# A scheduler that writes the order of work for one core: new durations, a lock between two engines, and one load per block

## The chip, the core and the metric

The kernel runs on one core of a Trainium2 chip. The core has five engines that each run their own list of instructions in the order in which the program was built: TensorE (PE, matrix products; its weight loads are shown as PEld), VectorE (DVE), ScalarE (ACT), GpSimd (POOL) and SyncE (SP), which here only issues DMAs. ACT issues some DMAs too, on a queue of its own. An engine waits when its next instruction needs a result that is not there yet, and everything behind that instruction on the same engine waits with it. The metric is the device time of one execution in microseconds (us), as the median of several runs.

## What is computed

Queries, keys and values are float32, the weights float64; the result is float32. First an attention over 4 batches, 8 heads, 576 positions and 64 values a head, which is the sum of a pooled part (queries, keys and values averaged in groups of four, 144 by 144 scores a head) and a local part (each position sees its neighbours at a distance under four). Then two feed-forward stages on 2304 tokens. In short:

```python
out_d = sm_attn(q_d, k_d, v_d)             # pooled by 4
out_up = np.repeat(out_d, factor, axis=2)
mask = np.abs(pos[:, None] - pos[None, :]) < factor
out_local = softmax(where(mask, q @ k.T / 8, -1e9)) @ v
x = out_up + out_local                     # 2304 x 512
h = x @ w_in                               # 512 -> 2048
x = (h * np.cos(h)) @ w_out                # 2048 -> 512
a = x @ w1;  b = x @ w2                    # 512 -> 1024
out = (a * b @ w3) @ w_out2                # 1024 -> 1024 -> 512
```

## The kernel before

The program is not written in the order in which it runs. It consists of small jobs (generators), each with an urgency, that ask for one operation after the other on a named engine. The function `run` (line 271) plays the kernel through once while it is being built: it keeps a clock, and whenever an engine is free it gives it the most urgent operation whose inputs are visible. `cost` (line 89) says how long an operation takes, `LATENCY` (line 67) how long until others see its result. The order of instructions that comes out of this game is what the chip then runs. So a change of a number in `cost` changes no operation; it changes which operation stands where in an engine's list.

The stages, by the names that the trace shows:

- Start: a batch's blocks of queries and keys are loaded (tiles `qb` and `kb`); two constants, `bands_in` and `ident_in`, come over ACT's own DMA queue (lines 1094 to 1096) and are turned into `ident_r` (line 1100), which the first local scores `ps_sb` need. Pooled sums `qkd` are made on VectorE and give the pooled scores `ps_s`. While TensorE has nothing to do, the scheduler puts products of zeros into its list (`ps_z`, and later into `ps_w`; `warm_up`, line 1058).
- `ps_w`: w3 times the last weights, 64 float32 products. The weights come as float64, and `w_job` (line 315) makes float32 of them: an ACT activation `t<-raw`, a VectorE shift `t<-t`, a VectorE or `w<-raw,t`; for later stages also an ACT copy and a GpSimd subtraction (`wi`, `wo`).
- `ps_h` and `ps_y`: the first feed-forward stage, 96 steps of 12 products each in both; between them `chain_job` (line 801) computes h cos h on ACT, VectorE and GpSimd. The attention of the later batches is threaded in: `ps_s`, `ps_t`, `ps_p` for the pooled part (`pair_job`, line 455), `ps_sb`, `ps_tb`, `ps_av` for the local part (`unit_job`, line 592; a unit is two blocks of 96 positions).
- `ps_ab` and `ps_o`: the second stage.

The functions that the change touches are `cost`, the `issue` inside `Engine`, `unit_qk_job` (line 417: loads for the first batch) and `unit_job` (line 592: loads for the other batches, and the scores).

Of the kernel before, what the change touches and what calls it, by code (L numbers as in the profile page):

```python
# [21 lines left out]
P = 128  # L22
# [10 lines left out]
KB = QB + 2 * HALO  # L33
NQB = S // QB
# [24 lines left out]
AHEAD = 12  # L59
A0, A1 = 6.0, 6  # L60
# [6 lines left out]
LATENCY = {"pe": 200, "se": 140, "ve": 130, "ge": 150, "sy": 2450}  # L67
# [9 lines left out]
def fused_kernel(ctx: ExitStack, tc: tile.TileContext, qk_block, v_block, qk_pool, v_pool,  # L77
# [6 lines left out]
    written, table = {}, [AF.Exp]  # L84

    def size(a):
        return math.prod(a.shape[1:])

    def cost(name, op, out, ins, func):
        n = max(size(a) for a in [out] + ins)  # L90
        if name == "ve":
            shared = n > 64 and ends["ge"] > max(now[0], ends["ve"])
            if op.startswith("tensor_scalar") and len(ins) == 1:
                return 90 + n * (1.5 if shared else 0.65)
            both = len(ins) == 2 and n > 64 and not any(a.tensor.name.startswith("ps_") for a in ins)
            return 75 + n * (2.2 if both and shared else 1.17 if both else 1.04)
        if name == "se":
            load = 1283 if func in (AF.Exp, AF.Sin) and func != table[0] else 0
            table[0] = func if load else table[0]
            return (60 if ins[0].tensor.name.startswith("ps_") else 100) + n / 1.2 + load  # L100
        if name == "ge":
            return 160 + (1.7 if any(0 in [step for step, _ in a.ap] for a in ins) else 2.3) * n
        if name == "sy":
            return max(450, n * out.shape[0] * (8 if out.dtype == I64 else 4) / 290)
        n = size(out)
        if op == "transpose":
            return 70
        if ins[0].dtype == F32R:
            return 12.5 + n / 2.4
        quarters = ins[0].shape[0] == D and size(ins[0]) == D  # L110
        return (4 if ins[0].shape[0] == P else 1 if quarters else 2) * max(35, n / 2.4)
# [6 lines left out]
    class Engine:  # L118
# [3 lines left out]
        def __getattr__(self, op):  # L122
            call = getattr(self.engine, op)

            def issue(*args, **kw):
# [9 lines left out]
                end = ends[self.name] = max(now[0], ends[self.name]) + cost(self.name, op, out, ins, kw.get("func")) + (0 if also is None else 183)  # L135
# [75 lines left out]
    def on(name, fn, *aps, when=lambda: True):  # L211
        yield name, fn, aps, when
# [203 lines left out]

    def unit_qk_job(u):
# [3 lines left out]
        unit_qk[u] = qs, ks  # L421
# [7 lines left out]
        yield from on("ve", lambda: ve.tensor_reduce(out=pooled[:, :, 0, ub * n:(ub + 1) * n], in_=qs[1].rearrange("p n (g r) -> p n g r", r=4), axis=AX.X, op=ALU.add), qs[1])  # L429
        for side in range(2):  # L430
            g = ub * n + side * n // 2
            yield from on("ve", lambda: ve.tensor_reduce(out=pooled[:, :, 1, g:g + n // 2], in_=ks[1][:, side, :KC * KB].rearrange("p (n k) -> p n k", n=KC)[:, :, HALO:HALO + QB].rearrange("p n (g r) -> p n g r", r=4), axis=AX.X, op=ALU.add), ks[1])
        count(("pooled", b))
# [158 lines left out]
    def unit_job(u):  # L592
# [8 lines left out]
        if early:  # L601
            yield from until(lambda: u in unit_qk)
            qk_slots, (qs, ks) = zip(*unit_qk.pop(u))
        else:
            qk_slots = yield from take("raw", 2)
            qs, ks = buf(qk_slots[0], "qb", [KC, UQ]), buf(qk_slots[1], "kb", [2, 512])
            for side in range(2):
                yield from on("sy", lambda: sy.dma_start(out=qs[:, :, side * QB:(side + 1) * QB], in_=qk_block[2 * u + side, :, :KC * QB].rearrange("p (n q) -> p n q", n=KC)))
            yield from on("sy", lambda: sy.dma_start(out=ks[:, :, :KC * KB], in_=qk_block[2 * u:2 * u + 2, :, KC * QB:].rearrange("b p n -> p b n")))
# [3 lines left out]
        def scores():  # L613

            for s0, s1, kind in masks_of(u):
# [4 lines left out]
                for side in range(s0, s1):  # L620
                    for m in range(2):
                        for w in range(2):
                            for c in range(2):
                                for r in range(2):
                                    rs, o = slice(r * D, (r + 1) * D), ((side * 2 + m) * 2 + w) * KS
                                    q0, k0 = side * QB + w * (QB - KS), (2 * m + c) * KB + w * (KB - KS)
                                    pe.matmul(ps[r][c * KS:(c + 1) * KS, o:o + KS], lhsT=qs[rs, 2 * m + c, q0:q0 + KS], rhs=ks[rs, side, k0:k0 + KS],
                                              start=u >= BANDS, stop=u >= BANDS or (side, m, w) == (s1 - 1, 1, 1))

        yield from on("pe", scores, qs, ks, bands, ident_r)  # L630
# [558 lines left out]
```

## Time and profile before

| what | value |
|---|---|
| median of 3 runs | 844.81 us (844.55 to 844.94) |
| the profiled execution, device time | 845.89 us |
| its span, first to last instruction | 844.1 us, 15707 instructions |
| PE busy | 827.9 us, 98% of the span |
| DVE, ACT, POOL busy | 517.3, 451.1, 372.7 us |
| granted TensorE clock, mean | 0.997 of full speed |
| DMA | 121.88 MB in 61403 packets, 18960 of them under 512 B |
| table loads on ACT | 28 of 1283 ns |

The span is the stretch that the profile covers; the device time of the same execution is 1.79 us longer, and that execution was 1.08 us above the median. Busy times of the engines overlap each other and don't add up to the span. In a timeline row a group of equal instructions that follow each other is merged; neighbouring groups on PE overlap by 0.1 to 0.2 us, since products are pipelined. A float32 product shows up as two records.

### The profile page before, as it was taken

The page shows a single profiled execution, that of the slowest core. Times are in us where ns is not written, and L with a number is a line of the kernel's source. Part 1 is how long each engine was busy: PE and PEld are TensorE (multiplying, and loading weights), DVE is VectorE, ACT ScalarE, POOL GpSimd, SP SyncE. Part 2 cuts the span into 40 slices and gives each one's busy share as a digit, 9 for nine tenths or more (in the row PEclk, how much of TensorE's full clock was granted, in tenths as well). Part 3 has the DMA queues.
Part 4 walks back from the last instruction along what each step waited for, and adds up shares of the span by engine and source line. Part 5 has one row for each costly group of instructions (what it writes and reads, how often), then busy time and mean ns, then how long its engine had stood idle before and what let it go on. Part 6 is the DMA issues. An engine that isn't in the chain of part 4 may idle for free.

```text
span 844.1 us, 15707 instructions
## 1 busy us (share of the span) xinstructions
PE 827.9 (98%) x5982; PEld 751.1 (89%) x5982; DVE 517.3 (61%) x924; ACT 451.1 (53%) x906; POOL 372.7 (44%) x330
## 2 busy tenths in 40 slices
PE   8999999999999999999999999999999999999997
PEld 7544599999989999999999999999999899999996
DVE  6888789998777678757453442654436544463342
ACT  2646698877778767857775565551214211231111
POOL 0102559865454533634443433444435632363332
PEclk9999999999999999999999999999999999999999
DMA  9997897134453545353332144968002400020102
GB/s 271 295 316 269 278 309 289 40 116 130 139 162 136 187 126 171 106 164 103 103 124 99 64 140 156 365 223 339 26 14 62 138 26 25 26 88 26 26 26 75
DMA packets 61403, 121.88 MB, mean 144 GB/s; under 512 B 18960, under 2 KB 26384, under 8 KB 61328
## 3 DMA queue, kind: packets, MB, share of 16 engines
q1 hardware_dynamic: 54432, 112.12, 41.0%
q10 hardware_dynamic: 6896, 8.76, 3.0%
q8 instruction: 47, 0.77, 0.4%
q14 instruction: 28, 0.23, 0.1%
HBM read 93.07 MB, written 27.79 MB: 143 GB/s over the span
## 4 chain that ended last, share of the span: by engine, by line
PE 81%; DVE 8%; DMA 6%; ACT 3%; issue 1%; POOL 1%; ACTq 0%; DVEq 0%; POOLq 0%
PE ps_ab L138 20%; PE ps_y L138 18%; PE ps_h L138 18%; PE ps_o L138 12%; PE ps_w L138 7%; DVE t L138 3%; DMA raw<-w_out 2%; PE ps_t L138 2%; DVE c L138 1%; DMA raw<-w_in 1%; PE ps_av L138 1%; PE ps_tb L138 1%; PE ps_sb L138 1%; PE ps_s L138 1%; DMA vr<-v_pool 1%
## 5 line engine op out<-in xcount | busy, mean ns | idle before, releaser
L138 PE MATMUL ps_y<-g,wo 128*128 128x384 f32 x1152 | 221.2, 337 | 0.5 <-POOL g L138 0.5
L138 PE MATMUL ps_h<-xs,wi 128*128 128x384 f32 x1152 | 220.6, 337 | 1.1 <-POOL wi L138 1.1
L138 PEld LDWEIGHTS ps_h<-xs,wi 128*128 128x128 f32 x1152 | 200.1, 188 | 5.2 <-issue 2.4
L138 PEld LDWEIGHTS ps_y<-g,wo 128*128 128x128 f32 x1152 | 199.9, 188 | 3.0 <-issue 1.4
L138 PE MATMUL ps_ab<-y,w 128*128 128x384 f32 x1008 | 185.1, 336 | 0.9 <-DVE v L138 0.8
L138 PEld LDWEIGHTS ps_ab<-y,w 128*128 128x128 f32 x1008 | 176.8, 188 | 6.5 <-issue 1.4
L138 DVE TENSOR_TENSOR v<-v,ps_ab 128x384 f32<-128x384 f32 x168 | 90.8, 552 | 136.8 <-ACT w L138 70.4
L138 POOL TENSOR_TENSOR g<-c,g 128x384 fp32r<-128x384 f32 x96 | 108.5, 1131 | 137.6 <-ACT g L138 125.6
L138 ACT ACTIVATE c<-c 128x384 f32<-128x384 f32 x192 | 100.4, 523 | 30.1 <-DVE c L138 27.6
L138 POOL TENSOR_TENSOR v<-v 128x384 f32<-128x384 f32 x48 | 49.8, 1039 | 140.9 <-DVE v L138 139.1
L138 PE MATMUL ps_o<-w,m 128*128 128x512 f32 x432 | 107.3, 392 | 0.0
L138 ACT CAST m<-v 128x384 fp32r<-128x384 f32 x48 | 24.5, 514 | 141.0 <-POOL v L138 141.0
L138 DVE SCALAR_TENSOR_TENSOR c<-turns,ps_h 128x384 f32<-128x384 int32 x96 | 52.6, 548 | 67.1 <-ACT turns L138 61.0
L138 PEld LDWEIGHTS ps_o<-w,m 128*128 128x128 f32 x432 | 80.3, 188 | 14.1
L138 DVE SCALAR_TENSOR_TENSOR c<-c,ps_h 128x384 f32<-128x384 f32 x96 | 52.6, 548 | 45.5 <-ACT c L138 45.2
L138 ACT ACTIVATE turns<-ps_h 128x384 int32<-128x384 f32 x96 | 47.0, 489 | 42.9 <-PE ps_h L138 42.6
L138 ACT CAST g<-c 128x384 fp32r<-128x384 f32 x96 | 49.2, 512 | 37.3 <-DVE c L138 31.3
L138 PE MATMUL ps_w<-w,w 128*128 128x512 f32 x128 | 61.1, 617 | 1.0 <-DVE w L138 1.0
L138 DVE TENSOR_SCALAR t<-t 128x512 int32<-128x512 int32 x72 | 49.7, 704 | 10.0 <-ACT t L138 10.0
L138 ACT ACTIVATE t<-raw 128x512 f32<-128x512 f32 x72 | 47.7, 675 | 13.9 <-DMA raw<-w 6.0
L138 POOL TENSOR_TENSOR m<-v,m 128x384 fp32r<-128x384 f32 x48 | 47.8, 1017 | 0.0
L138 POOL TENSOR_TENSOR xs<-xb,xs 128x384 fp32r<-128x384 f32 x24 | 26.9, 1122 | 47.2 <-ACT xs L138 47.1
(89 smaller groups left out, 866.3 us busy)
## 6 DMA issues: line engine op xcount, KB each, us to landing
w_sc<-w SPq DMA_DIRECT2D x56, 256.0 KB
w<-w_sc SPq DMA_DIRECT2D x28, 512.0 KB
raw<-w SPq DMA_DIRECT2D x24, 512.0 KB
raw<-w3t SPq DMA_DIRECT2D x16, 512.0 KB
raw<-w_in SPq DMA_DIRECT2D x16, 512.0 KB
raw<-w_out SPq DMA_DIRECT2D x16, 512.0 KB
qkr<-qk_pool SPq DMA_DIRECT2D x12, 576.0 KB
vb<-v_block SPq DMA_DIRECT2D x48, 128.0 KB
```

The lines of the kernel that those rows point to most:

```text
L138: return call(*args, **kw)
```

## The change

Three things are changed.

1. A block's queries and keys (they lie side by side in DRAM, 792 values per partition) come in one DMA into one tile `qk`, where before queries of two blocks went into `qb`, 96 values at a time, by two DMAs, and keys of two blocks into `kb` by a third. The function `halves` gives the two views of the new tile. In the first batch each VectorE sum of `qkd` over 768 values becomes two over 384.
2. The table in `cost`, the latencies and the DMA rate have other numbers. One line of it stands here for all.
3. The scheduler's game knows a lock between VectorE and GpSimd (`held`): a GpSimd `tensor_tensor` and a VectorE operation that works from SBUF to SBUF with two inputs (or a `tensor_scalar`) wait for each other there. It also adds a price for TensorE's change between products with few and with many rows. These are prices in the game; no instruction is added for them.

```diff
+QK = KC * (QB + KB)
+RATE = 310
-LATENCY = {"pe": 200, "se": 140, "ve": 130, "ge": 150, "sy": 2450}
+LATENCY = {"pe": 200, "se": 145, "ve": 115, "ge": 120, "sy": 2450}
+    def held(name, op, out, ins, start):
+        if name == "ge" and op == "tensor_tensor":
+            return max(0.0, lock["ve"] - 60 - start)
+        if name == "ve" and size(out) > 64 and on_chip(out) and all(on_chip(a) for a in ins) and (len(ins) == 2 or op.startswith("tensor_scalar")):
+            return max(0.0, lock["ge"] - 110 - start)
+        return None
-            return 160 + (1.7 if any(0 in [step for step, _ in a.ap] for a in ins) else 2.3) * n
+            return (160 + 1.66 * n) if any(0 in [step for step, _ in a.ap] for a in ins) else 132 + 2.18 * n
...
-                end = ends[self.name] = max(now[0], ends[self.name]) + cost(self.name, op, out, ins, kw.get("func")) + (0 if also is None else 183)
+                start = max(now[0], ends[self.name])
+                wait = held(self.name, op, out, ins, start)
+                if self.name == "pe":
+                    part = op == "matmul" and ins[0].shape[0] <= QP and ins[0].dtype == F32
+                    start += 0 if part == parts[0] else 120 if part else 200
+                    parts[0] = part
+                end = ends[self.name] = start + (wait or 0) + cost(self.name, op, out, ins, kw.get("func")) + (0 if also is None else 190)
+                if wait is not None:
+                    lock[self.name] = end
...
-        qs = yield from load(lambda t: [(t[:, :, side * QB:(side + 1) * QB], qk_block[2 * u + side, :, :KC * QB].rearrange("p (n q) -> p n q", n=KC)) for side in range(2)], "w", ANY, "qb", (KC, UQ), F32)
-        ks = yield from load(lambda t: [(t[:, :, :KC * KB], qk_block[2 * u:2 * u + 2, :, KC * QB:].rearrange("b p n -> p b n"))], "w", ANY, "kb", (2, 512), F32)
+        for side in range(2):
+            got.append((yield from load(qk_block[2 * u + side], "w", ANY, "qk", (QK,), F32)))
...
+            g, (qs, ks) = ub * n + side * n // 2, halves(got[side][1])
+            for which, src in enumerate((qs, ks[:, :, HALO:HALO + QB])):
+                yield from on("ve", lambda: ve.tensor_reduce(out=pooled[:, :, which, g:g + n // 2], in_=src.rearrange("p n (g r) -> p n g r", r=4), axis=AX.X, op=ALU.add), src)
```

The order of instructions changes on every engine. Over the whole program TensorE keeps its 76 products `ps_z` and loses the 12 products of zeros `ps_w<-zeros`; the other products are the same in number. The table loads on ACT become 20. The places that matter below:

First place, VectorE while the second unit's scores come in (`sc` are local scores, `bmax` their maxima or sums, `nm` and `sums` and `sd` belong to a pooled pair, `vr` and `vd` to pooled values, `t` and `w` to weights). Before:

```order
L138 TENSOR_TENSOR vr<-vr 72x2x256
L138 TENSOR_TENSOR sc<-ps_sb,bmax 128x512
L138 TENSOR_TENSOR vd<-vr 72x256
L138 TENSOR_REDUCE bmax<-ps_sb 128x8
L138 TENSOR_REDUCE nm<-ps_s 72x2 x2
L138 TENSOR_REDUCE bmax<-sc 128x16
L138 TENSOR_SCALAR nm<-nm 72x4
L138 TENSOR_SCALAR t<-t 128x512
```

and now:

```order
L160 TENSOR_TENSOR vr<-vr 72x2x256
L160 TENSOR_REDUCE bmax<-ps_sb 128x8
L160 TENSOR_TENSOR vd<-vr 72x256
L160 TENSOR_TENSOR sc<-ps_sb,bmax 128x512
L160 TENSOR_REDUCE bmax<-ps_sb 128x8
L160 TENSOR_SCALAR t<-t 128x512
L160 TENSOR_TENSOR sc<-ps_sb,bmax 128x512
L160 TENSOR_REDUCE nm<-ps_s 72x2 x2
L160 TENSOR_REDUCE bmax<-sc 128x16
L160 TENSOR_SCALAR nm<-nm 72x4
L160 SCALAR_TENSOR_TENSOR w_323<-raw,t 128x512
```

The subtraction `sc<-ps_sb,bmax` of the second unit's first half now stands ahead of `nm`, and the first weight's `or` ahead of the division of `bmax`.

Second place, VectorE right behind that, up to the second weight, which the first `ps_w` needs. Before:

```order
L138 TENSOR_SCALAR bmax<-bmax 128x16
L138 RECIPROCAL bmax<-bmax 128x16
L138 SCALAR_TENSOR_TENSOR w_342<-raw,t 128x512
L138 TENSOR_SCALAR t<-t 128x512
L138 TENSOR_SCALAR sums<-sums 72x4
L138 RECIPROCAL sums<-sums 72x4
L138 SCALAR_TENSOR_TENSOR w_361<-raw,t 128x512
L138 TENSOR_TENSOR sd<-sd,sums 72x576
```

and now:

```order
L160 TENSOR_SCALAR bmax<-bmax 128x16
L160 RECIPROCAL bmax<-bmax 128x16
L160 TENSOR_SCALAR t<-t 128x512
L160 TENSOR_REDUCE bmax<-ps_sb 128x8
L160 TENSOR_SCALAR sums<-sums 72x4
L160 RECIPROCAL sums<-sums 72x4
L160 TENSOR_REDUCE nm<-ps_s 72x2
L160 TENSOR_TENSOR sd<-sd,sums 72x576
L160 TENSOR_REDUCE nm<-ps_s 72x2
L160 SCALAR_TENSOR_TENSOR w_358<-raw,t 128x512
```

Two `nm`, one `bmax` and the product `sd<-sd,sums` have moved ahead of the second weight's `or`.

Third place, TensorE from the first `ps_w` on. Before:

```order
L138 MATMUL ps_w_375<-w_342,w_361 128x512
L138 MATMUL ps_w_389<-w_342,w_361 128x512
L138 MATMUL ps_w_394<-w_342,w_361 128x512
L138 MATMUL ps_w_400<-w_342,w_361 128x512
L138 MATMUL ps_w_375<-zeros 128x256
L138 MATMUL ps_t<-ident,sd 72x72 x8
L138 MATMUL ps_tb<-ident,sc 128x128 x8
L138 MATMUL ps_w_375<-zeros 128x256 x5
L138 MATMUL ps_t<-ident,sd 72x72 x8
L138 MATMUL ps_t<-ptp,vd 64x144 x4
L138 MATMUL ps_s<-qkd 72x144 x4
L138 MATMUL ps_w_375<-zeros 128x256
```

and now:

```order
L160 MATMUL ps_w_394<-w_323,w_358 128x512
L160 MATMUL ps_t<-ident,sd 72x72 x8
L160 MATMUL ps_w_403<-w_323,w_358 128x512
L160 MATMUL ps_tb<-ident,sc 128x128 x8
L160 MATMUL ps_s<-qkd 72x144 x4
L160 MATMUL ps_w_428<-w_323,w_358 128x512
L160 MATMUL ps_t<-ident,sd 72x72 x8
L160 MATMUL ps_t<-ptp,vd 64x144 x4
L160 MATMUL ps_w_467<-w_323,w_358 128x512
L160 MATMUL ps_w_394<-w_409,w_423 128x512
L160 MATMUL ps_s<-qkd 72x144 x4
```

The twelve products of zeros in this stretch are gone (seven of them stand in the rows of before), and transposes and pooled scores stand between the first products `ps_w`.

## Rows read from the trace of the kernel before

**Rows 1.** Stretches: us, busy us of PE, PEld, DVE, ACT, POOL; PEclk, DMA share, GB/s
```profile
0.00:24.00 24.00, 18.63 (x227) 16.14 (x227) 15.79 (x29) 7.39 (x17) 2.80 (x7) 0.99 0.97 266
24.00:104.00 80.00, 80.00 (x637) 42.12 (x637) 67.71 (x150) 48.69 (x132) 20.13 (x14) 0.98 0.91 293
104.00:155.00 51.00, 49.20 (x348) 46.56 (x347) 45.92 (x68) 46.94 (x93) 40.28 (x29) 1.00 0.77 255
155.00:200.00 45.00, 43.14 (x363) 41.98 (x362) 42.61 (x60) 35.20 (x67) 31.85 (x23) 1.00 0.30 91
200.00:560.00 360.00, 358.31 (x2963) 345.71 (x2962) 220.63 (x401) 246.81 (x477) 162.58 (x145) 1.00 0.45 146
560.00:840.00 280.00, 278.64 (x1454) 258.57 (x1452) 124.53 (x220) 65.73 (x123) 115.02 (x113) 1.00 0.22 77
```

**Rows 2.** What PE waited for: us in total, times, longest us
```profile
PE ps_sb L138 <- DVE sc L138: 1.3, 1, 1.3
PE ps_tb L138 <- DVE sums L138: 1.3, 1, 1.3
PE ps_sb L138 <- ACT ident_r L138: 1.1, 1, 1.1
PE ps_h L138 <- POOL wi L138: 1.1, 2, 0.8
```

**Rows 3.** PE in order of time: start us, us, operation, idle before it
```profile
23.90 5.24 PE L138 MATMUL ps_w<-w,w 128*128 128x512 f32 x8 [1.01 <-DVE w L138]
30.39 0.84 PE L138 MATMUL ps_w<-zeros 128*128 128x256 f32 x5
31.07 0.67 PE L138 MATMUL ps_t<-ident,sd 72*72 72x72 f32 x8
31.66 0.71 PE L138 MATMUL ps_t<-ptp,vd 72*64 72x144 f32 x8
40.66 4.89 PE L138 MATMUL ps_w<-w,w 128*128 128x512 f32 x11
```

**Rows 4.** The first 24 us on ACT, DVE and POOL in order of time
```profile
0.74 2.62 ACTq L132 DMA_DIRECT2D bands_raw<-bands_in  x4
8.46 0.31 ACT L138 ACTIVATE ident_r<-ident 128x128 fp32r<-128x128 f32 x1
11.06 0.69 DVE L138 TENSOR_REDUCE bmax<-ps_sb 128x8 f32<-128x512 f32 x1 [1.24 <-PE ps_sb L138]
19.62 0.42 DVE L138 TENSOR_SCALAR t<-t 128x512 int32<-128x512 int32 x1
20.55 2.15 POOL L138 TENSOR_TENSOR sc<-sc,bmax 128x1024 f32<-128x1024 f32 x1 [19.37 <-DVE bmax L138]
20.87 2.12 DVE L138 TENSOR_SCALAR t<-t 128x512 int32<-128x512 int32 x1
23.19 0.66 DVE L138 SCALAR_TENSOR_TENSOR w<-raw,t 128x512 int32<-128x512 int32 x1
```

**Rows 5.** VectorE's groups: count, busy us, mean ns, idle before
```profile
L138 DVE TENSOR_REDUCE nm<-ps_s 72x2 f32<-72x288 f32 x32 | 13.7, 448 | 10.2 <-PE ps_s L138 10.1
L138 DVE TENSOR_TENSOR sd<-sd,sums 72x576 f32<-72x576 f32 x8 | 6.0, 749 | 0.0
L138 DVE TENSOR_TENSOR sc<-ps_sb,bmax 128x512 f32<-128x512 f32 x4 | 2.7, 680 | 0.0
```

**Rows 6.** DMA queues, 566.8 to 574 us: packets, MB, share of 16 engines
```profile
q1 hardware_dynamic: 600, 2.19, 74.5%
q10 hardware_dynamic: 575, 0.79, 29.4%
```

**Rows 7.** Three stretches at the start, columns as in rows 1
```profile
1.70:4.20 2.50, 2.50 (x13) 2.50 (x13) 0.00 (x0) 0.00 (x0) 0.00 (x0) 1.00 0.94 194
23.60:27.00 3.40, 3.10 (x4) 1.51 (x5) 3.40 (x9) 1.64 (x6) 0.00 (x0) 0.50 1.02 324
24.00:60.00 36.00, 36.00 (x282) 19.64 (x283) 30.91 (x71) 20.63 (x56) 1.90 (x1) 0.96 1.03 309
```

More of the change, by code (lines that the diff above doesn't have):

```diff
@@ L83, in fused_kernel, with on_chip @@
     ends = {"ve": 0.0, "se": 0.0, "pe": 0.0, "ge": 0.0, "sy": 0.0}
-    written, table = {}, [AF.Exp]
+    written, table, lock, parts = {}, [AF.Exp], {"ve": 0.0, "ge": 0.0}, [False]
     def size(a):
         return math.prod(a.shape[1:])
+    def on_chip(a):
+        return not a.tensor.name.startswith("ps_")
+    def held(name, op, out, ins, start):
[4 more added lines that the diff above has]
+        return None
     def cost(name, op, out, ins, func):
@@ L91, in cost @@
         if name == "ve":
[L92 to L96, printed above, removed]
+            if n <= 64:
+                return 80 if op != "tensor_scalar_add" else 190
+            if len(ins) == 1 and op.startswith("tensor_scalar") and on_chip(ins[0]):
+                return 68 + 0.52 * n
+            return 64 + 1.043 * n
         if name == "se":
-            load = 1283 if func in (AF.Exp, AF.Sin) and func != table[0] else 0
+            load = 1290 if func in (AF.Exp, AF.Sin) and func != table[0] else 0
             table[0] = func if load else table[0]
-            return (60 if ins[0].tensor.name.startswith("ps_") else 100) + n / 1.2 + load
+            return (45 if not on_chip(ins[0]) else 128 if func == AF.Prelu else 90) + n / 1.2 + load
         if name == "ge":
-            return 160 + (1.7 if any(0 in [step for step, _ in a.ap] for a in ins) else 2.3) * n
+            return (160 + 1.66 * n) if any(0 in [step for step, _ in a.ap] for a in ins) else 132 + 2.18 * n
         if name == "sy":
-            return max(450, n * out.shape[0] * (8 if out.dtype == I64 else 4) / 290)
+            return max(450, n * out.shape[0] * (8 if out.dtype == I64 else 4) / RATE)
         n = size(out)
         if op == "transpose":
-            return 70
+            return 109 if out.shape[0] == P else 62
         if ins[0].dtype == F32R:
-            return 12.5 + n / 2.4
+            return 13.3 + n / 2.4
         quarters = ins[0].shape[0] == D and size(ins[0]) == D
-        return (4 if ins[0].shape[0] == P else 1 if quarters else 2) * max(35, n / 2.4)
+        return (4 if ins[0].shape[0] == P else 1 if quarters else 2) * max(30, n / 2.4)
     def visible(a):
@@ L602, in unit_job @@
             yield from until(lambda: u in unit_qk)
-            qk_slots, (qs, ks) = zip(*unit_qk.pop(u))
+            qk_slots, qk = zip(*unit_qk.pop(u))
         else:
             qk_slots = yield from take("raw", 2)
-            qs, ks = buf(qk_slots[0], "qb", [KC, UQ]), buf(qk_slots[1], "kb", [2, 512])
+            qk = [buf(slot, "qk", [QK]) for slot in qk_slots]
             for side in range(2):
-                yield from on("sy", lambda: sy.dma_start(out=qs[:, :, side * QB:(side + 1) * QB], in_=qk_block[2 * u + side, :, :KC * QB].rearrange("p (n q) -> p n q", n=KC)))
-            yield from on("sy", lambda: sy.dma_start(out=ks[:, :, :KC * KB], in_=qk_block[2 * u:2 * u + 2, :, KC * QB:].rearrange("b p n -> p b n")))
+                yield from on("sy", lambda: sy.dma_start(out=qk[side], in_=qk_block[2 * u + side]))
+        qs, ks = zip(*(halves(t) for t in qk))
         ns = yield from banks(2)
@@ L625, in scores @@
                                     rs, o = slice(r * D, (r + 1) * D), ((side * 2 + m) * 2 + w) * KS
-                                    q0, k0 = side * QB + w * (QB - KS), (2 * m + c) * KB + w * (KB - KS)
-                                    pe.matmul(ps[r][c * KS:(c + 1) * KS, o:o + KS], lhsT=qs[rs, 2 * m + c, q0:q0 + KS], rhs=ks[rs, side, k0:k0 + KS],
+                                    q0, k0 = w * (QB - KS), w * (KB - KS)
+                                    pe.matmul(ps[r][c * KS:(c + 1) * KS, o:o + KS], lhsT=qs[side][rs, 2 * m + c, q0:q0 + KS], rhs=ks[side][rs, 2 * m + c, k0:k0 + KS],
                                               start=u >= BANDS, stop=u >= BANDS or (side, m, w) == (s1 - 1, 1, 1))
-        yield from on("pe", scores, qs, ks, bands, ident_r)
+        yield from on("pe", scores, *qk, bands, ident_r)
         for s in qk_slots:
```

8 lines of the change are left out of this document (4 added, 4 removed).

## The prediction

> **What bounds the kernel now.** I first read the table by stretches [rows 1]: the reader is to see that TensorE (PE) is busy for all of 24 to 104 us, for 49.20 of 51 us and 43.14 of 45 us in the two stretches behind that, and nearly always from 200 us on. Its idle time is 5.37 us before 24 us, then 1.80, 1.86, 1.69 and 1.36 us. No other engine comes near it over the whole, though VectorE is busy for 42.61 of 45 us from 155 to 200 us, and ACT for 46.94 of 51 us from 104 to 155 us. The products of after are those of before, apart from twelve products of zeros. So the time can move in three ways only: the moment from which PE has real work without a break, the products of zeros, and the 6.7 us of idle time (1.80 + 1.86 + 1.69 + 1.36) behind 24 us. Then I read what PE waited for [rows 2]: single waits of 0.3 to 1.3 us on results of VectorE, ACT and GpSimd, none directly on a DMA. Last I read the start in order of time [rows 3, 4], since the two places of the change that touch it, the loads and VectorE's order, both stand before the first `ps_w` at 23.90 us.
>
> **The start, VectorE's order.** In before the first maximum `bmax<-ps_sb` starts at 11.06 us, when PE's first scores are there [rows 4], and VectorE works without a break until the second weight's `or`, which starts at 23.19 and takes 0.66 us; PE starts `ps_w` with it [rows 3, 4]. The change moves four operations ahead of that `or`. First the subtraction `sc<-ps_sb,bmax` (0.68 us, about 0.6 behind its neighbour), and the first `or` ahead of the division, which shifts the second `t<-t` by about 0.7 in all. Then the lock: in before the second `t<-t` starts at 20.87, just after GpSimd began a 2.15 us product at 20.55, and takes 2.12 us, against 0.42 us for the same operation at 19.62 [rows 4]. From its start to the end of the `or` are 3.0 us. In the new order it follows the division directly and gets in first, 0.4 us; but `sd<-sd,sums`, which has two inputs in SBUF, now stands behind it and must wait out the 2.15 us; with its own 0.75, half of a pair of `nm` (0.45 each) and the `or`, 0.66, that is 4.3 us from the start of `t` [rows 4, 5]. So +0.7 and +1.3: the first `ps_w` starts about 2.0 us later, at 25.9 us, if the scores come as early as before.
>
> **The start, the first rows of zeros and transposes.** From 23.90 to 40.66 us PE works through two rounds of four products `ps_w` and what is between them, 16.8 us [rows 3]. Of this the new order lacks the products of zeros (five step from 30.39 to 31.07, 0.14 each, twelve are 1.6 us), and one pair of `ps_t` and `ps_t<-ptp`, 1.2 us, which comes later instead. In before the clock was at 0.50, the lower of its two levels (1.2 GHz), from 23.6 to 27.0 us [rows 7]: eight records of `ps_w` took 5.24 us, against 4.89 for eleven at 40.66 [rows 3], so about 1.6 us were lost. If the clock holds in after, the stretch takes 16.8 - 1.6 - 1.2 - 1.6 = 12.4 us and the third round starts at 25.9 + 12.4 = 38.3, where before, with the pair taken off, stood at 39.5. That is 1.2 us won; since VectorE also has to finish the third round's weights by then, with one more wait for the lock, I take 1.0.
>
> **The start, the loads.** The first scores need `ident_r`, which ACT makes at 8.46 us, as soon as its constants have landed [rows 4]; PE waited 1.1 us for it [rows 2]. These constants come on ACT's queue in 896 rows of 128 to 384 B (four DMAs of 192 rows, then 96 and 32), 56 on each of 16 DMA engines, beside SP's queue. Where both queues were full, from 566.8 to 574 us, they moved 600 and 575 packets: as many of the one as of the other, though a row of SP's was more than twice as large [rows 6]. In before SP's rows at the start are 384 and 1632 B long, and the DMA engines move 194 GB/s; with rows of 2 KB and more they move 309 GB/s [rows 7]. After the change SP's rows are 3168 B, five times the mean of before (811 KB in 1280 rows for two blocks), and SP's queue never runs dry, as each DMA has 128 rows instead of 256 to 512. If each of the 56 rows takes turns with one of SP's, the constants wait for 56 x 16 x (3168 + 256) B = 3.07 MB at 309 GB/s, 9.9 us from about 2.4 us on (the first of the four is issued from 0.74 to 1.4 us, and SP's first bytes too moved about 1 us behind their issue), and some 0.4 to land. `ident_r` would be made at 12.7 instead of 8.46, 4.2 us later. The other bound is zero: the queue of constants is not held up at all; better than now can't pay, as VectorE's sums fill that time. No row of before shows rows of 3168 B beside these, so the value is an estimate; I take 3.3, as the equal counts are the nearest row. The loads themselves land earlier, by 2.4 MB x (1/194 - 1/309) = 4.6 us at most, but that buys nothing here, since VectorE then stands before `bmax<-ps_sb` with six sums done and must wait for PE.
>
> The Trainium skill, "DMA: Bandwidth & Descriptors", section "Queues, rings and completion order", says that a DMA engine takes turns between queues by whole packets of some 9 to 17 descriptors. By that rule the six DMAs of constants would each wait for one share of a block, 8 rows on each engine, 1.3 us; with 0.7 us for their own bytes that is 8.6 us instead of 9.9, a delay near 2.9 us and a sum lower by 0.4. Counts as in these rows can't tell the two apart.
>
> Start in sum: -1.0 + 3.3 = +2.3 us for all that follows, since PE has no gap until 104 us in which it could catch up.
>
> **The stretch from 104 to 200 us.** The 3.66 us of idle time here are waits for `wi`, `g` and freed banks behind VectorE, ACT and GpSimd, which are nearly full because they convert weights [rows 1, 2]. Their work does not hang on PE's start, so with PE 2.3 us later they are ahead by about that much. I take 2.2 of the 3.66 us back. The 20 table loads instead of 28 take 10 us from ACT, which helps in the same place and counts in it. **From 200 us on** the order is new but of the same kind; of 3.05 us idle I take 0.4 off, with bounds of 1.5 to both sides, since the two long waits there (1.3 us for `sums` is one) may go or come again. The chain at the end is unchanged: the last ten or eleven products `ps_o` cover the last weights' chain in both. The larger loads of later units are hidden, PE waits for no load there now; without that cover each would cost what it lands late, some tenths. The six sums more on VectorE at the start add 6 x 0.05 us at most, and lie before `bmax`.
>
> **Sum.** Against the profiled execution's 845.89 us: +2.3 - 2.2 - 0.4 = 845.6; that execution was 1.08 us above the median, so the forecast for the median is 844.5 us. A measurement of this kernel tells about 0.2%, 1.7 us, from no change; this is no change.
>
> **Rivals.**
> - Faster: the constants land as early as now (delay 0). For it: the new SP DMAs issue fewer rows, so the queue of constants may be served sooner; against it: the equal counts of rows 6. Then -1.0 - 2.2 - 0.4 = -3.6 us, 841.2 us; if all waits behind 104 us went too, 837 us. Chance 0.30.
> - Slower, by one mechanism: the constants come late, PE runs out of zeros at 7 us and stands until 12 us, and as after its half-idle stretch before 23.6 us it gets the lower clock for its first real work. For it: the drop in rows 7; against it: the first real work is mostly paced by VectorE, not by PE. Price: delay 4.2, scores at half clock 1.2, first `ps_w` at half clock 1.6: -1.0 + 4.2 + 2.8 - 2.6 = +3.4, 848.2 us. It decides from delay and clock together above 5.3 us. Chance 0.18.
> - The new order makes waits of its own: after 155 us the second `ps_sb` stands closer behind the first, before VectorE has freed its banks, which cost 1.3 us once already. Twice that more than forecast: 847.1 us. Chance 0.10.
> - The table does nothing on the chip: the lock is still there, the game only knows of it. Then the waits behind 104 us stay as they are and the sum is +2.3, 847.1; a part of this lies in the forecast's spread, and no chance of its own is given.
>
> **How the numbers follow.** Forecast 0.42, the rivals 0.30, 0.18 and 0.10. The forecast's own range is 842.3 to 846.5. The range over all cases goes from 840.8, which takes in half of the faster rival's cases, to 848.4, which takes in the slower ones but the worst. Faster 0.31, same 0.41, slower 0.28: the faster rival and a sliver of the forecast's tail, the forecast, and the two slower ones.
>
> **What would show it.** `ident_r` on ACT at 11 to 13 us instead of 8.46, with an idle time of 3 us or more on PE before the first `ps_sb`; the first `ps_w` at 28 to 30 us and no product of zeros behind it; `sd<-sd,sums` locked beside GpSimd's product instead of `t<-t`; PE idle for under 2 us between 104 and 200. It would be wrong if `ident_r` stands at 9 us (then faster), or if the first `ps_w` starts after 31 us or the granted clock falls to the lower level in the scores (then slower).

## The result, and the profile after

The changed kernel takes 850.13 us in the median of 6 runs (849.11 to 852.48), the kernel before 844.88 (844.55 to 845.61): a ratio of 1.0062, with a 95% interval of 1.0049 to 1.0075. It is slower by 0.6%; 844.5 and no change had been forecast. The profiled execution of after took 849.11 us with a span of 847.2, 3.1 us more than that of before.

The table by stretches, columns as in [rows 1], is that of after. Two single rows follow it: the time from the first `ps_h` to the end, first in before, then in after.

```profile
0.00:24.00 24.00, 19.47 (x215) 16.90 (x215) 14.09 (x30) 6.52 (x15) 0.98 (x7) 0.86 0.93 296
24.00:104.00 80.00, 77.89 (x637) 41.09 (x634) 77.46 (x159) 51.50 (x139) 26.72 (x18) 1.00 0.92 303
104.00:155.00 51.00, 46.44 (x332) 43.87 (x331) 43.65 (x61) 42.16 (x85) 37.11 (x27) 1.00 0.61 223
155.00:200.00 45.00, 44.60 (x374) 43.69 (x373) 40.82 (x62) 34.92 (x67) 30.62 (x23) 1.00 0.29 93
...
```
```profile
103.97:844.10 740.13, 729.33 (x5122) 692.86 (x5120) 433.79 (x748) 395.08 (x758) 349.74 (x309) 1.00 0.38 124
```
```profile
106.48:847.20 740.72, 728.51 (x5106) 692.43 (x5104) 424.67 (x737) 382.07 (x742) 344.88 (x306) 1.00 0.36 121
```

The reader is to see three things. PE's granted clock over the first 24 us is 0.86 instead of 0.99. From 104 to 155 us PE is idle for 51 - 46.44 = 4.56 us instead of 1.80, and from 155 to 200 us for 0.40 instead of 1.86. And the 3.1 us split at the first `ps_h`: it comes 2.5 us later, 0.8 us less work is left behind it, and PE is idle 12.2 us from there to the end instead of 10.8. So in this execution 1.7 us were lost before and 1.4 us behind that product.

What PE waited for, as in [rows 2]. The two waits of 1.3 us for VectorE are gone, those for `ident_r` and the second weight `w` are about 1 us longer, and waits for ACT (`up`, `pt`) are new:

```profile
PE ps_tb L160 <- ACT up L160: 2.2, 1, 2.2
PE ps_w L160 <- DVE w L160: 2.1, 1, 2.1
PE ps_sb L160 <- ACT ident_r L160: 2.0, 1, 2.0
...
PE ps_h L160 <- ACT pt L160: 1.1, 1, 1.1
```

The start in order of time (ACT, then VectorE and GpSimd, then PE), which answers to [rows 3, 4]:

```profile
9.13 0.31 ACT L160 ACTIVATE ident_r<-ident 128x128 fp32r<-128x128 f32 x1 [0.58 <-DMA ident<-ident_in]
...
12.92 0.69 DVE L160 TENSOR_REDUCE bmax<-ps_sb 128x8 f32<-128x512 f32 x1 [4.48 <-PE ps_sb L160]
...
23.45 0.36 DVE L160 TENSOR_SCALAR t<-t 128x512 int32<-128x512 int32 x1
...
24.32 1.29 DVE L160 TENSOR_SCALAR sums<-sums 72x4 f32<-72x4 f32 x1
...
26.09 0.74 DVE L160 TENSOR_TENSOR sd<-sd,sums 72x576 f32<-72x576 f32 x1
...
27.12 0.68 DVE L160 SCALAR_TENSOR_TENSOR w<-raw,t 128x512 int32<-128x512 int32 x1
...
23.68 1.91 POOL L160 TENSOR_TENSOR sc<-sc,bmax 128x1024 f32<-128x1024 f32 x1 [22.49 <-DVE bmax L160]
...
9.49 0.53 PE L160 MATMUL ps_sb<-bands,ident_r 128*128 128x256 f32 x2 [1.97 <-ACT ident_r L160]
...
27.85 1.13 PE L160 MATMUL ps_w<-w,w 128*128 128x512 f32 x2 [2.10 <-DVE w L160]
```

And ACT beside PE behind 102 us, where no row of before stood:

```profile
103.54 0.35 ACTq L146 DMA_DIRECT2D w_sc<-w  x1
104.12 1.06 ACT L160 ACTIVATE sc<-sc 128x1024 f32<-128x1024 f32 x1 [0.61 <-DVE sc L160]
105.08 1.05 ACT L160 COPY w<-ps_w 128x512 f32<-128x512 f32 x2
...
106.59 0.69 ACT L160 COPY ptp<-ps_t 72x288 f32<-72x288 f32 x2 [0.46 <-PE ps_t L160]
111.71 0.59 ACT L160 COPY w<-ps_w 128x512 f32<-128x512 f32 x1 [4.43 <-DMA w_sc<-w]
112.20 0.30 ACT L160 ACTIVATE up<-ps_t 128x144 f32<-128x144 f32 x1
...
112.55 0.66 PE L160 MATMUL ps_tb<-ident,sc 128*128 128x128 f32 x4 [2.23 <-ACT up L160]
```

The fourth copy of the weights' product waits for a buffer that an earlier copy's store still holds. That store was issued at 103.54, and ACT goes on at 111.71, 8.2 us later; `cost` and `LATENCY` give a store 0.07 + 0.85 + 2.45 = 3.4 us. All that stands behind the copy on ACT, `up` above all, is late, and PE waits. Before anything is tested this is a reading of the rows; e3, e10 and e13 below test it.

### The profile page after: what moved, and what is told of

It reads as the page before. It is cut to its first block, busy times and chain, and to the rows that moved or that the text cites. A ratio compares the mean times of both kernels' runs of the same rounds, so it can differ in the third digit from the quotient of the medians.

```text
span 847.2 us, 15623 instructions
## 1 busy us (share of the span) xinstructions
PE 828.4 (98%) x5970; PEld 751.8 (89%) x5970; DVE 517.9 (61%) x927; ACT 442.1 (52%) x898; POOL 372.6 (44%) x330
## 4 chain that ended last, share of the span: by engine, by line
PE 71%; DVE 4%; ACT 2%; DMA 2%; issue 1%; POOL 1%; ACTq 0%; DVEq 0%; POOLq 0%; SPq 0%
PE ps_ab L160 20%; PE ps_y L160 18%; PE ps_h L160 17%; PE ps_o L160 12%; DVE bmax L160 1%; DMA raw<-w 1%; PE ps_av L160 1%; PE ps_t L160 1%; DVE c L160 1%; DVE sc L160 1%; PE ps_sb L160 1%; PE ps_tb L160 1%; PE ps_s L160 1%; DVE t L160 1%; DMA part_sc<-yt 0%
## 5 line engine op out<-in xcount | busy, mean ns | idle before, releaser
L160 PE MATMUL ps_ab<-y,w 128*128 128x384 f32 x1008 | 188.9, 337 | 0.6 <-ACT v L160 0.5
L160 POOL TENSOR_TENSOR g<-c,g 128x384 fp32r<-128x384 f32 x96 | 105.8, 1103 | 156.5 <-ACT g L160 145.6
L160 PE MATMUL ps_o<-w,m 128*128 128x512 f32 x432 | 110.9, 393 | 0.0
L160 DVE TENSOR_SCALAR t<-t 128x512 int32<-128x512 int32 x72 | 52.3, 741 | 9.3 <-ACT t L160 9.3
L160 PEld LDWEIGHTS ps_w<-w,w 128*128 128x128 f32 x128 | 22.8, 189 | 26.2 <-issue 22.5
## 6 DMA issues: line engine op xcount, KB each, us to landing
raw<-w3t SPq DMA_DIRECT2D x16, 512.0 KB, 10.8
```

The lines of the kernel that those rows point to most:

```text
L160: return call(*args, **kw)
```

## Experiments

Medians of 4 to 12 runs, each with the ratio to runs of the kernel before that were taken beside it (their median was 844.7 to 845.7 us). "Clock" is the mean granted clock over the runs; PE's idle time from 104 to 155 us and the first `ps_w` are those of the profiled execution.

| run | us | ratio (95%) | clock | first `ps_w` | idle 104-155 |
|---|---|---|---|---|---|
| before | 844.9 | 1 | 0.998 | 23.90 | 1.80 |
| after | 850.13 | 1.0062 (1.0049-1.0075) | 0.993 | 27.85 | 4.56 |
| e9 after again | 849.53 | 1.0058 (1.0043-1.0073) | 0.994 | 27.62 | 3.15 |
| e1 loads alone | 849.02 | 1.0047 (1.0029-1.0065) | 0.995 | 25.68 | 2.15 |
| e2 table and lock alone | 853.89 | 1.0109 (1.0089-1.0129) | 0.992 | 25.54 | 7.17 |
| e10 e2, spare buffer | 849.30 | 1.0068 (1.0045-1.0091) | 0.996 | 25.71 | 2.95 |
| e3 spare buffer | 847.91 | 1.0030 (1.0016-1.0043) | 0.995 | 27.55 | 1.87 |
| e4 zeros, first pause | 848.59 | 1.0051 (1.0032-1.0070) | 0.996 | 26.69 | 3.71 |
| e5 e3 and e4 | 848.88 | 1.0043 (1.0028-1.0059) | 0.996 | 27.30 | 2.83 |
| e6 e3, zeros in all pauses | 846.48 | 1.0016 (1.0004-1.0029) | 0.999 | 27.11 | 2.29 |
| e13 store counted longer | 846.51 | 1.0020 (1.0006-1.0033) | 0.995 | 27.53 | 0.71 |
| e16 e13, zeros in all pauses | 845.78 | 0.9999 (0.9987-1.0010) | 1.000 | 27.44 | 0.70 |
| e7 before, zeros | 846.03 | 1.0010 (0.9996-1.0024) | 0.999 | 25.03 | 2.02 |
| e14 before, fewer zeros | 844.52 | 0.9994 (0.9980-1.0008) | 0.999 | 23.83 | 1.80 |
| e8 no lock in the book | 875.81 | 1.0359 (1.0338-1.0380) | 0.985 | 28.53 | 6.43 |
| e11 old book to 30 us | 857.55 | 1.0140 (1.0118-1.0162) | 0.991 | 25.07 | 3.47 |
| e12 e11, zeros | 854.60 | 1.0117 (1.0099-1.0136) | 0.995 | 25.42 | 4.67 |
| e15 e13, small locks, zeros | 849.02 | 1.0042 (1.0025-1.0059) | 0.994 | 27.36 | 4.74 |

**e1 and e2: the two halves.** e1 is the diff's hunks on `qk` alone, e2 all of its others.

> The kernel before with the one load of queries and keys alone; table of durations and lock as before. Theory A (the loss of the whole change is two things: TensorE stands about 2 us ahead of the first scores, so that they run at the lower level of its clock, and ACT waits 4.4 us for a store of the product of the two weights at 107 us): the start loses its part here too, ident_r at 9.0 to 9.3 us, granted clock near 0.5 in the scores, first maximum at 12.5 to 13 us, but the order at 107 us is another; 846.0 to 847.5 us. Rival B (the larger loads do it all, by their traffic): 849 to 850.5 us. Rival C (the new order of the scheduler does it all): 844.5 to 845.5 us.

> The changed kernel with the loads of before (two tiles, qb and kb); new table of durations and lock. Theory A: ident_r at 8.46 us as before, granted clock 1.0 in the scores, first maximum at 11.1 us; ACT still waits for a store of the product of the weights near 107 us, as its copies stand close to the stores in this order too, so 847 to 848.5 us. Rival B (the loads): 844.5 to 845.5 us. Rival C (the order): 849 to 850.5 us.

Both halves are slower by themselves, by 0.47% and 1.09%, and together they lose 0.62%: they do not add, since each writes an order of its own. e1 lies in B's range, but e2, with the loads of before, is worse than any theory had it, so B falls, and C falls with e1. The starts came as theory A had them: in e1 `ident_r` at 9.33, a clock of 0.77 from 9.5 to 17 us and `bmax` at 12.79; in e2 a clock of 1.00 there and `bmax` at 11.31.

In e1's profiled execution the loss is one of clock: PE is idle for 1.2 us less than in before (848.1 - 833.1 = 15.0 against 844.1 - 827.9 = 16.2), with a wait of 2.1 us for `g` among it, but busy for 5.2 us longer with as many products, at a mean clock of 0.989. That is the lowest of its seven; over all seven the times go from 846.04 at a clock of 1.000 to 850.96 at 0.992. In e2 ACT waits for a store, too (ACT's wait, then PE's behind it):

```profile
ACT w L159 <- DMA w_sc<-w: 4.3, 1, 4.3
...
PE ps_y L159 <- POOL g L159: 7.2, 1, 7.2
```

**e3, e10: a buffer that no store holds.** In e3 the order is that of after, word for word.

```diff
-        w = buf(slot, "w5", [512])
+        w = buf(("st", 0) if f == F2 - 1 else slot, "w5", [512])
```

> The changed kernel, every engine's order the same, but the eighth copy of the product of the two weights goes to a buffer that is idle then, so that it does not wait for the store of an earlier copy. Theory A: ACT's 4.4 us wait at 107 us is gone, up and pt come earlier, TensorE is idle for at most 2.0 us between 104 and 155 us instead of 4.56, and the time falls by 2.5 to 2.9 us, to 847.2 to 847.7. Rival D (ACT has too much to do there, the wait for the store only takes up its slack): idle time in this stretch stays above 3.8 us and the time above 849.3 us.

> The kernel of e2 (new table and lock, loads of before), order the same, but its second copy of the later four rows of the weights' product, the one that waited 4.35 us for a store, goes to an idle buffer. Theory A (a wait for a store stops ACT and all behind it): ACT's wait goes, TensorE's wait of 7.17 us for g falls under 3.5 us, the time falls by 3.5 to 5 us, to 849 to 850.4 us. Rival D (ACT's load is what lasts; the wait only fills its slack): over 852.5 us.

e3 gains 1.6 us on after as run again in e9 (2.2 on its first median), less than the 2.5 expected; by the two ratios, which take out how fast before was beside each, it is 2.4. e10 gains 4.6 us on e2, as expected (3.5 by the ratios). The rows are e3's third stretch and e10's wait for `g`:

```profile
104.00:155.00 51.00, 49.13 (x343) 45.84 (x342) 46.40 (x63) 44.16 (x88) 39.47 (x29) 1.00 0.63 236
```
```profile
PE ps_y L159 <- POOL g L159: 3.0, 1, 3.0
```

In both orders the other operations stand as they did and the wait for the store is a cost, not slack.

**e9: the changed kernel again.**

> The changed kernel as it is, beside the others on this chip, so that differences to it do not rest on another session: 849.5 to 850.6 us; if it is under 849 us, the gains so far told against 850.13 us (spare buffer, zeros) have to be cut by as much.

It repeats. Its profiled execution, which is also its median, has a longer first pause and a shorter wait for `up`:

```profile
PE ps_sb L160 <- ACT ident_r L160: 3.2, 1, 3.2
...
PE ps_tb L160 <- ACT up L160: 0.9, 1, 0.9
```

It loses in another place than the profiled execution of after. The next rows are its stretch from 24 to 104 us, which stood at a clock of 1.00 in after, two of its PE rows from there, and its first `ps_h`:

```profile
24.00:104.00 80.00, 77.91 (x630) 41.52 (x630) 75.13 (x159) 51.57 (x136) 25.78 (x18) 0.98 0.94 300
```
```profile
29.20 2.01 PE L160 MATMUL ps_w<-w,w 128*128 128x512 f32 x2
31.00 1.71 PE L160 MATMUL ps_tb<-ident,sc 128*128 128x128 f32 x8
...
108.22 3.40 PE L160 MATMUL ps_h<-xs,wi 128*128 128x384 f32 x18
```

From 29 to 32 us the granted clock is 0.50 (two `ps_w` records 2.01 us instead of 1.07), and the first `ps_h` comes 1.7 us later than in after. Split as above, 3.8 us are lost before it, and behind it PE is idle 10.5 us, 0.3 less than in before. The store does not follow PE: where PE comes later to 104 us, less of the wait is left. That fits e3, which gives less back than the 2.8 us which the profile of after shows.

**e4, e5, e6: zeros in PE's pauses.** The order is after's; `zeros(n)` issues n products `ps_z`, past the scheduler's book. The diff is that of e6, without its definition of `zeros`: ahead of the first scores, inside the first two `ps_s`, and ahead of the first `ps_w`. e4 and e5 have the first of these places alone, with 18; e5 and e6 also have e3's buffer.

```diff
+            zeros(20 if u == 0 else 0)
             for s0, s1, kind in masks_of(u):
...
+                    if b == 0 and (c, r) == (0, 1):
+                        zeros({0: 16, 1: 12}.get(p, 0))
...
+                    yield from on("pe", lambda: (zeros(16 if (r, j, e) == (0, 0, 0) else 0), pe.matmul(ps[e], lhsT=wa[:, es].bitcast(F32), rhs=w.bitcast(F32), start=j == 0, stop=j == F2 - 1)), w, wa)
```

> The changed kernel, order the same, with 18 more products of zeros (0.11 us each) right ahead of the first scores, so that TensorE works on while ident_r is not there. Theory A (the pause of 1.97 us is what takes the clock down): granted clock 1.0 from 9.5 to 17 us, first maximum at 11.0 to 11.3 us instead of 12.92, first ps_w 1.5 to 2.0 us earlier, time 848.1 to 848.7 us, and the runs closer to each other. Rival E (the lower clock comes in any case, a few us later, on the first ps_w as in the kernel before, or VectorE paces the stretch): first ps_w less than 0.7 us earlier, 849.6 to 850.5 us.

> The changed kernel with both single edits: the eighth copy of the weights' product in an idle buffer, and 18 products of zeros ahead of the first scores. Theory A (the two losses are independent): 2.2 us (spare buffer alone) and about 1.5 us (zeros alone) add up: 3.4 to 4.0 us under the changed kernel, 846 to 846.7 us; the clock still falls once between 18 and 28 us. Rival E (what the zeros win at the scores is lost again when the lower clock comes on the first ps_w): no better than the spare buffer alone, 847.5 to 848.3 us.

> The changed kernel with the spare buffer and zeros in all four pauses that TensorE has before 28 us (20 ahead of the first scores, 16 and 12 between the first and second product of the first two ps_s, 16 ahead of the first ps_w); order the same. Theory A (the lower clock follows TensorE's pauses, and makes up about 3.8 us of the 5.2): mean granted clock at or above 0.998 in most runs, no stretch at 0.50 before 60 us, 844.0 to 845.5 us, within 0.1 per cent of the kernel before. Rival F (the lower clock comes whatever TensorE does, by the chip's own state): mean clock 0.994 to 0.996 as with the spare buffer alone, 847 to 848.5 us.

The next rows are the scores in before, in after and in e4, then 19 to 27 us in e4:

```profile
9.50:17.00 7.50, 6.41 (x157) 5.30 (x148) 6.26 (x12) 0.13 (x1) 0.00 (x0) 1.00 1.08 324
```
```profile
9.50:17.00 7.50, 7.50 (x140) 6.11 (x141) 4.08 (x9) 0.68 (x1) 0.00 (x0) 0.54 1.01 366
```
```profile
9.50:17.00 7.50, 6.83 (x155) 5.56 (x155) 5.22 (x11) 0.67 (x1) 0.00 (x0) 1.00 1.03 371
19.00:27.00 8.00, 7.32 (x34) 5.98 (x34) 7.93 (x18) 4.70 (x15) 1.90 (x1) 0.57 1.05 291
```

With the pause of 1.97 us filled, the scores run at the upper level (2.4 GHz) and `bmax` starts at 11.78 instead of 12.92; but behind the next pauses (1.69 us for `sc` is one) the clock falls to the lower level from 19 us on. So e4 won the scores, as theory A had it, and lost the clock a few us later, as rival E had it; e5 is not told apart from e3. Only with all four pauses filled (e6) is the mean clock 0.999. e6 is 1.4 us better than e3, but the two intervals overlap, and 846.48 is 1 us above the range of its theory A; the gain of the zeros shows clearly only in e16 below.

The length of the pause does not settle the price. From the start of `ident_r` to that of `bmax` it is 2.6 us in before, and 2.6 in every changed kernel whose pause was filled. With a pause (its length in brackets) it was 3.8 in after (1.97), 3.5 in e1 (1.73) and 4.1 in e8 (2.75), but 2.9 to 3.2 in e3, e9 and e13 (3.2 to 3.3), and 2.6 in e10 (2.25) and e11 (3.04), where the clock fell at 18 to 19 us instead.

**e7, e14: the same in the kernel before** (10, 8, 8, 10 zeros; then 8, 5, 1, 7).

> The kernel before with zeros in its pauses before 24 us (10, 8, 8 and 10 products in the same four places). Theory A: its mean granted clock of 0.998 goes to 1.000, no stretch at 0.62 from 24 to 28 us, and it gains what that lost, 1 to 2 us: 843.0 to 844.0 us. Rival F: no gain, 844.5 to 845.5 us.

> The kernel before, with as many zeros as its pauses before 24 us hold and no more (8, 5, 1 and 7). Theory A (zeros win the clock and cost only where they are longer than the pause): first ps_w at 23.8 to 24.2 us (25.03 with 10, 8, 8 and 10), mean clock 0.999, 843.2 to 844.4 us. Rival F (the clock is worth nothing in the start, since VectorE paces it): 844.6 to 845.6 us.

Longer zeros than the pauses delayed the first `ps_w` by 1.1 us, and e7 won nothing. Fitted, they raised the clock as expected, and the first `ps_h` came 1.3 us earlier (102.66), but no gain shows in the time: 0.9994, with an interval that excludes more than 0.2%. A gain of 1.3 us is inside that interval, so whether the lower clock on before's first `ps_w` [rows 7] costs anything stays open.

**e8: durations without the lock** (`wait = None` in place of `held(...)`).

> The changed kernel without the lock in the scheduler's book (durations and loads as changed). Its order puts sd ahead of t<-t again on VectorE and has the fourth copy of the weights' product behind another set of operations. Theory A (the loss comes from where the order happens to put that copy and from the start, not from the lock): start as in the changed kernel, at most 1 us of ACT's waiting for the store; 847 to 848.5 us. Rival G (knowing the lock costs nothing or helps; the durations are at fault): 849.5 to 851 us. Rival H (the lock itself is the fault): 844 to 846 us.

All three were wrong by far: 875.81 us. The old durations of VectorE held an allowance for GpSimd; the new ones leave it to the lock. Without it the book takes VectorE for faster than it is next to GpSimd, and PE stands still for results of both. That the one is the cause of the other was not tested further. PE's waits:

```profile
PE ps_y L160 <- POOL g L160: 8.5, 5, 2.3
PE ps_s L160 <- DVE qkd L160: 5.5, 3, 5.0
PE ps_h L160 <- DVE c L160: 3.1, 2, 2.4
```

**e11, e12: VectorE's old order at the start.** Up to 30 us of the scheduler's clock the old durations and no lock, with e3's buffer; in e12 with zeros (18, 12, 8, 4).

> The changed kernel with the spare buffer, and with the old durations of VectorE and GpSimd and no lock in the scheduler's book up to 30 us of its clock; the new ones from there. VectorE makes the second weight in the order of before (its second t<-t, one subtraction, then the or, and sums and sd behind it). Theory A (VectorE's new order costs 2 us at the start): first ps_w at 24.3 to 25.5 us instead of 27 to 28; 845.0 to 846.5 us. Rival I (the gain at the start is lost again before 155 us, as VectorE has no idle time there): first ps_w as told, but 847.5 to 849 us.

> The kernel of e11 with zeros in TensorE's pauses at the start as well (18, 12, 8 and 4). Theory A: mean granted clock at or above 0.998, 0.5 to 1.5 us faster than e11, 844 to 845.5 us, no slower than the kernel before. Rival F (the zeros delay VectorE's chain by what they win in clock, as they did in the kernel before): within 0.5 us of e11.

The first `ps_w` came at 25.07, 2.5 us earlier than in e3, as theory A had it, and the first `ps_h` at 107.97, no earlier than in e3 (108.10). Then a load that had not landed took the place of the store (ACT, then PE, of e11):

```profile
114.28 0.67 ACT L175 ACTIVATE t<-raw 128x512 f32<-128x512 f32 x1 [3.13 <-DMA raw<-w_in]
...
117.53 6.05 PE L175 MATMUL ps_h<-xs,wi 128*128 128x384 f32 x24 [3.47 <-ACT ptp L175]
```

So rival I was right in that the gain is lost again, and far too mild; the one wait of 3.5 us is not the whole of it. The profiled execution (853.10) is the fastest of the five, and what the others lost beyond it is not known. e12's zeros raised the mean clock to 0.995, not to the 0.998 of its theory A; it is 3.0 us below e11, with intervals that overlap.

**e13, e15, e16: the store's time in the book.**

```diff
-        give_stored("t", slot, w5_sc[f])
+        free["t"].append((visible(w5_sc[f]) + 4000, slot))
```

> The changed kernel, whose scheduler counts 4 us more until the buffer of a stored row of the weights' product is free again; the order is a new one from the first such row on (64 us). Theory A (what was wrong is the time that the scheduler's book gives a store; the buffer is only another cure): no wait of ACT for a store from 100 to 115 us and 847 to 848.5 us, as with the spare buffer. Rival J (each new order brings waits of its own, and the cure of one says little of the whole): the wait is gone and the time is 848.5 us or more, with TensorE idle over 3 us between 104 and 155 us on other results.

> As e13, and the scheduler also counts the lock for VectorE's small TENSOR_SCALAR operations (sums<-sums took 1.29 instead of 0.16 us beside GpSimd's product), with zeros in the pauses at the start (18, 12, 8, 6). Theory A (better numbers give a better order): 844 to 846 us, no slower than the kernel before. Rival J (a truer book does not make a shorter program here, the order is a draw): 847 us or more, with a new wait of over 2 us on TensorE between 104 and 200 us.

> The kernel of e13 (the scheduler gives a store 4 us more) with zeros in TensorE's pauses at the start (20, 16, 12 and 16, as in e6). Theory A (the two losses, the wait for the store and the pauses with the lower clock behind them, make up the whole of what the change lost): the gains of e13 (about 3.3 us) and of the zeros (1.4 us) add up, mean clock at or above 0.999, 844.6 to 845.6 us, within 0.1 per cent of the kernel before. Rival F (the zeros only move the loss): within 0.6 us of e13, 846 us or more.

e13 has no wait of ACT for a store there; PE is idle for 0.7 us between 104 and 155, and the time falls by 3.0 to 3.6 us, to 0.5 us under the range of theory A. With the zeros on top (e16) nothing of the loss is left: 0.9999 of before, 0.9987 to 1.0010. Its 845.78 us are 0.2 above theory A's range, but before itself stood at 845.65 beside it; by the ratios the zeros gain 1.8 us here, where rival F allowed 0.6. Rows of e13, then of e16:

```profile
104.00:155.00 51.00, 50.29 (x353) 47.59 (x352) 46.88 (x62) 43.95 (x89) 37.41 (x28) 1.00 0.62 232
```
```profile
0.00:24.00 24.00, 22.11 (x263) 19.83 (x263) 14.73 (x31) 7.15 (x17) 1.63 (x7) 1.00 0.92 288
...
104.00:155.00 51.00, 50.30 (x360) 48.58 (x359) 47.89 (x63) 44.64 (x91) 38.53 (x29) 1.00 0.59 217
```

In e16 the first `ps_h` comes 2.0 us later than in before, and from there to the end PE is idle for 8.0 us instead of 10.8:

```profile
105.97 3.40 PE L160 MATMUL ps_h<-xs,wi 128*128 128x384 f32 x18
```

e15 tells the scheduler one more truth, the lock on small operations, and is 2.5 us slower than e13, and 3.2 slower than e16, which has zeros as well: PE waits 3.5 us for `c` behind 104 us. A truer book gave a worse order, as rival J had it. No version of the changed kernel beat the kernel before.

## Why the prediction was wrong

- **VectorE's order at the start: right.** From the first `bmax` to the start of the second `or` before the first `ps_w` it takes 14.20 us in after (12.92 to 27.12) against 12.13 in before; +2.07, forecast +2.0. The same 14.2 us stand in e6. The lock fell on `sums<-sums` (1.29 us instead of 0.15) and not on `sd<-sd`, which costs the same.
- **The constants: mis-sized.** `ident_r` came 0.67 us later (8.46 to 9.13), where 3.3 was taken with bounds of 0 and 4.2. In the twelve other profiled executions with these loads it stood at 9.18 to 9.81, in all five with the loads of before at 8.39 to 8.71, so the delay is 0.4 to 1.4 us. The equal counts of [rows 6] held at first: from 2 to 6 us SP's queue moved 385 packets and ACT's 402. From 6 to 8 us they were 154 and 554, and the constants were nearly through. The rule of the Trainium skill that the prediction weighed ("DMA: Bandwidth & Descriptors", section "Queues, rings and completion order") gave an estimate of 2.9, and isn't borne out here either.
- **The clock on the scores: in the slower rival, not in the forecast.** That rival had the pause and the lower clock behind it as one mechanism, with a delay of 4.2 us. The delay was small, and the clock fell all the same behind a pause of 1.97 us: from `ident_r` to `bmax` 3.79 us instead of 2.60, a price of 1.2 as that rival said. So the first `ps_w` came at 0.67 + 1.19 + 2.07 = 3.9 us later, 27.85, near the 28 to 30 named. That nearness is luck: a delay taken 2.6 us too long stood in for a lower clock of 1.2 us that the forecast had left out. Two signs of being wrong came true at once, `ident_r` at 9 us (then faster) and the lower clock in the scores (then slower).
- **From there to the first `ps_h`: right only where the clock held.** No zeros stood behind the first `ps_w`. The forecast let this part save 3.0 us, if the clock held; with 0.8 us less work left behind it, it saved 2.3 in the profiled execution of after, at a clock of 1.00, and nothing in e9, where the clock was 0.50 from 29 to 32 us. All of the start was forecast at +2.3; it is +1.7 in the profiled execution of after and +3.8 in that of e9.
- **From 104 us on: the step that failed.** "Their work does not hang on PE's start, so with PE 2.3 us later they are ahead by about that much. I take 2.2 of the 3.66 us back", and 0.4 more behind. From the first `ps_h` on, -2.6 us was forecast; measured were +1.4 in after and -0.3 in e9. The two waits of 1.3 us did go ([rows 2] has no counterpart). What I left out is that the new order can put new waits on in-order engines, here a copy behind a store 8.2 us long, and from 200 us on one of 1.5 us for `pt`. The third rival, waits of the new order's own, had the kind, but in another place and at 1.3 us each. e3 and e13 show that the wait for the store is the cause of 1.6 to 3.6 us; e13 also moves other operations, so the upper figure is not the store's alone.
- **What was right in that step.** In e16, with the store counted longer and the pauses filled, the start costs +1.7 us and PE is idle 2.8 us less behind it: the +2.3 and -2.6 of the forecast, nearly. So the time was taken back in an order without the new wait; that the lead of the other engines is what did it, as the prediction argued, is not shown.
- **From the profiled execution to the median: 1.1 us were taken off, 1.0 had to be added.** The profiled execution of after had a mean clock of 0.995, the other five 0.991 to 0.994; that of e9 shows a second fall of the clock, at 29 us, which that of after lacks. So the median of after probably holds more of it, but where the other five lost their clock is not recorded. With the pauses filled (e6, e16) the mean clock is 0.999 and more. e16 shows that with the store and these pauses out of the way no loss is left, and no gain that can be measured: the change as a whole, with its fuller loads, does not make the kernel faster than before.
- **"The table does nothing on the chip": near the truth.** VectorE's locked groups did not shrink as a whole: `t<-t`, `sd<-sd` and `sums<-sums` took 49.7, 6.0 and 4.2 us in before and grew, while `t<-t,s` went from 5.8 to 3.4. VectorE's busy time is 517.9 us, where it was 517.3. The three in after:

```profile
L160 DVE TENSOR_SCALAR t<-t 128x512 int32<-128x512 int32 x72 | 52.3, 741 | 9.3 <-ACT t L160 9.3
...
L160 DVE TENSOR_TENSOR sd<-sd,sums 72x576 f32<-72x576 f32 x8 | 7.1, 882 | 0.0
...
L160 DVE TENSOR_SCALAR sums<-sums 72x4 f32<-72x4 f32 x16 | 6.6, 416 | 0.5 <-ACT sd L160 0.3
```

Still open is what e2 and e11 lost beside the waits shown, and why the clock falls behind one pause and not behind another.

## What to carry to other kernels

Where a change lets a scheduler write a new order, don't cost it by what the old order waited for: list each wait on a DMA or on a buffer behind a store in the new order, and hold the distance from that DMA's issue against what such a transfer takes in the trace, with the engines as busy as they are there. A pause of TensorE ahead of work that another engine waits for can cost more than its length, as the work behind it may run at half the clock (here 1.2 us behind a pause of 2.0, and from nothing to 1.5 us in other executions). Idle products in the pauses kept the clock up only when all of them were filled, and they must not outlast the pause: in before, those that did (e7) were 1.4 us slower by the ratios than those that fitted (e14), with intervals that overlap.

## What was not expected of the hardware

- A store of 256 KB took 8.2 us from its issue until its buffer was free (103.54 to 111.71), with the DMA engines busy for a share of 1.00 from 100 to 105 us; in before the first such store was issued at 100.11, at a share of 0.46, and the fourth copy went ahead at 105.16 without a wait. The Trainium skill, "DMA: Bandwidth & Descriptors", section "Latency and other measured facts", lays a DMA's fixed cost of some 2 us to the round trip to the memory. That is near the 2.45 us of the scheduler's book, and in this place a quarter of what was measured. Part of the rest is seen: from 103 to 106 us SP's queue moved 313 packets and ACT's none, and from 106 to 109 us they moved 255 and 94, the first of the 432 of ACT's three stores. In before the first store's 144 packets all moved from 100 to 102 us.
- VectorE's lock holds up small operations too: one of four columns (`sums<-sums`) took 1.29 us instead of 0.15 beside GpSimd's product, and ended at 25.61 with that product (25.59). The Trainium skill, "SBUF — State Buffer", section "SBUF: two separate sides", says that whoever starts first keeps the ports for the whole instruction; the trace agrees.
- Six DMAs with rows of 3168 B kept SP issuing until 8.37 us, 1.3 us for each, where ACT's four took 0.66 each [rows 4]; SP's next load was issued at 8.41. It is not the long rows alone: in before two DMAs `qb` with rows of 384 B, issued at 3.70, took 2.85 us. In after:

```profile
0.74 7.63 SPq L160 DMA_DIRECT2D qk<-qk_block  x6
```
